# Decode attention with a gated MLP on one core: the rest of w2 loaded last, its products summed with wo's, and other sizes for the last value parts

## The chip, the cores and the metric

One Trainium2 chip, of which the kernel uses one core. The metric is the device time of one execution in microseconds, the median of several runs; lower is better.

## The reference

One token x (512 numbers) goes through two branches, and a gate mixes them. All tensors are bf16.

```python
g = sigmoid((x * gate_w).sum(-1))
q = (x @ wq).reshape(32 heads, 128)
scores = einsum("hd,hkd->hk", q, k_cache) * 128 ** -0.5     # 32 heads x 4096 positions
o = einsum("hk,hkd->hd", softmax(scores), v_cache)
a = o.reshape(4096) @ wo                                    # 4096 x 512
h = relu(x @ w1 + b1) ** 2                                  # 512 x 1376
b = h @ w2 + b2                                             # 1376 x 512
out = g * a + (1 - g) * b
```

The key and value caches are 32 x 4096 x 128 each, 67 MB together. wq and wo have 4 MB each, w1 and w2 1.4 MB each.

## The kernel before

There is no scheduler: each engine's program is written out by hand, and semaphores order the engines.

**Tiles.** Four heads make one tile of 4 MB (128 partitions x 128 blocks of 128 numbers), so there are NT = 8 key tiles and 8 value tiles. All of them, and the MLP's weights ("m"), pass through a ring of five slots in SBUF, `ring`, in the order of `LOADS`: k0, k1, k2, v0, k3, v1, and so on to k7, v5, v6, m, v7. SyncE (SP) issues these loads in that order (L319 to L338); before each it waits until the tile that had the slot is used up. The last three value tiles are loaded in parts with a semaphore each; `PARTS` holds where they are cut. For the last one these are blocks 0, 40, 76, 108, 128: parts of 40, 36, 32 and 20 blocks. One block is 128 x 128 numbers of bf16, 32 KB. Behind the last value part SP issues the last four heads' rows of wo in two pieces, three heads and one head (L340), and at the very end the store of the result.

**Scores and probabilities.** VectorE (DVE) computes 20 of each 32 blocks' scores with a fused multiply and sum (L716). TensorE (PE) transposes the other blocks (L509) and multiplies them with q (L524), with ScalarE (ACT) copying between. The maximum over a head goes over PE and DVE, ACT takes the exponentials (L434) and their sums.

**Values.** `pv(u)` multiplies blocks of a value tile with the probabilities (L555) and sums them in PSUM. `norm` (L746) divides by the sum of probabilities and multiplies by the gate g; the result is `onorm`.

**The end of the program on PE.** After the value products of tile 6:

- `turn_a`, `spread_a`, `out_a`: the first 28 heads are turned over and multiplied with 22 of the 32 parts of their rows of wo (L585, 88 products into `acc`, which is pQ[:, 256:260]).
- `mlp_h`: first MLP layer. The 1376 hidden units are 10 columns of 128 and a rest of FR = 96; per column four products (L600) into `H`.
- `den` (L564), then `mlp_out`: second MLP layer, 44 products (L612) into a PSUM region of its own, `MO`. The last four use `w2b`, the 96 rows of the rest of w2. `mlp_out` waits for both loads of w2 (`s_w[1]`, `s_w[2]`) and for `hs`.
- `pv` of the last value tile, in four steps that are its four parts. Between the first and the second, `add_v` (L591) adds the sum of the other ten parts of wo, which DVE computes itself (L777, L781).
- `out_b`: the last four heads times their rows of wo (L621, 12 and 4 products into `acc`); then the transpose of the final result.

On DVE, `mlp_bias` and `mlp` add b1, square the positive part and multiply by 1 - g (`omg`, one number per partition) to give `hs` (L756, L761, L765). Behind the sums for wo come the reciprocal, the sum of `MO` and the bias (L817), `norm` of the last group, the sum with `acc` (L821) and a copy (L823).

**At the start** SP and GpSimd may go on with wo's loads once q is computed and the bias b1 has been turned into columns (`started`); b1 goes over PE (L468) and two DVE copies into `b1c` (L700, L701).

Of the kernel before, what the change touches and what calls it, by code (L numbers as in the profile page):

```python
# [5 lines left out]
def bass_gated_mix__gqa_block_cached__dense_activation_squared_relu__decode_kernel(  # L6
# [15 lines left out]
    fp32 = mybir.dt.float32  # L22
    bf16 = mybir.dt.bfloat16
    ALU = mybir.AluOpType
# [5 lines left out]
    DM = 512  # L30
    F = 1376
    FG = 10
    FR = F - FG * 128
    SCALE = float(D) ** -0.5


# [2 lines left out]
    NT = NH // R  # L39
    B = 4096 // P  # L40
# [16 lines left out]
    PV[NU - 2] = [NU - 3 * U, NU - 3 * U + 1]  # L57
    PV[NU] = list(range(NU - 3 * U + 2, NU - U))

    PARTS = {NT - 3: [0, 64, B], NT - 2: [0, 32, 64, 96, B], NT - 1: [0, 40, 76, 108, B]}  # L60

    GR = [(0, 8), (8, 16), (16, 24), (24, 28), (28, 32)]
    NG = len(GR)
# [7 lines left out]
    NA = 28  # L71
    NZ = NH - NA
    TS = [0, 3, NZ]
# [59 lines left out]
    with ctx:  # L133
        def sb(name, shape, dt):
            return ctx.enter_context(nc.sbuf_tensor(name, shape, dt))
# [4 lines left out]
        def sem(name):  # L140
            return ctx.enter_context(nc.semaphore(name))
# [3 lines left out]
        def held(kind, j=0):  # L145
            return ring[:, AT[kind, j] % SLOTS, :]
# [4 lines left out]
        W2, W3 = 4 * F, 4 * F + FG * DM  # L151
        w1_sb = held("m")[:, 0:W2].rearrange("p (t n) -> p t n", t=4)
        w2a = held("m")[:, W2:W3].rearrange("p (g n) -> p g n", g=FG)
        w2b = held("m")[0:FR, W3:W3 + DM]
        W4 = W3 + DM
        W5 = W4 + NZ * DM
        wob_sb = held("m")[:, W4:W5].rearrange("p (h n) -> p h n", h=NZ)
# [4 lines left out]
        start = ring[:, SLOTS - 1, :]  # L162
# [6 lines left out]
        xrow, grow, b1r, b2r = early(1, DM), early(1, DM), early(1, F), early(4, 128)  # L169
# [5 lines left out]
        xcol = sb("xcol", [128, 4], bf16)  # L175
        xcolf = sb("xcolf", [128, 4], fp32)
        b1c = sb("b1c", [128, FG + 1], fp32)
# [17 lines left out]
        onorm = sb("onorm", [128, NH], bf16)  # L195
# [4 lines left out]
        omg = sb("omg", [128, 1], fp32)  # L200
        hr = sb("hr", [128, FG + 1], fp32)
        hp = sb("hp", [128, FG + 1], fp32)
        hs = sb("hs", [128, FG + 1], bf16)
        b2g = sb("b2g", [128, 4], fp32)
        fin = sb("fin", [128, 4], bf16)

# [4 lines left out]
        pX = pb("pX", [128, 512], fp32)  # L211
# [9 lines left out]
        B2 = KP[2][:, 0:4]  # L221
        QR = [pQ, pX]
        H = pX[:, 256:256 + FG + 1]
        MO = pX[:, 288:292]
        B1 = pM[:, 288:288 + FG + 1]
        acc = pQ[:, 256:260]

# [50 lines left out]
        s_rd = sem("s_rd")  # L278
        s_on = sem("s_on")
        s_h = sem("s_h")  # L280
        s_mo = sem("s_mo")
        s_fb = sem("s_fb")
        s_vs = sem("s_vs")
        s_hv = sem("s_hv")
        s_hs = sem("s_hs")
# [25 lines left out]
        def started(eng):  # L311
            eng.wait_ge(s_qps, NT)
            eng.wait_ge(s_g, 4)
            eng.wait_ge(s_b1c, 2)


        @block.sync
        def _(eng):
            for n, (kind, j) in enumerate(LOADS):  # L319
                free(eng, n)  # L320
                if n == SLOTS - 1:
                    started(eng)
                    for p, st, k, q in STRIPS[len(RUNS):]:
                        a, b = W[p:p + st * (k - 1) + 1:st, :], woa_v[q:q + k, :]
                        if k == 1:
                            a, b = [v.rearrange("p (a n) -> p a n", a=2) for v in (a, b)]
                        eng.dma_start(a, b).then_inc(s_wr, 16)
                if kind == "v" and j in PARTS:
                    for w in range(len(PARTS[j]) - 1):
                        part = slice(PARTS[j][w] * 128, PARTS[j][w + 1] * 128)  # L330
                        eng.dma_start(held("v", j)[:, part], v_v[j][:, part]).then_inc(s_vl[j, w], 16)  # L331
                elif kind in "kv":
                    eng.dma_start(held(kind, j), (k_v if kind == "k" else v_v)[j])\
                       .then_inc(s_l[n % SLOTS], 16)
                elif kind == "m":
                    eng.dma_start(held("m")[:, 0:W2], w1_v).then_inc(s_w[0], 16)
                    eng.dma_start(held("m")[:, W2:W3], w2_v).then_inc(s_w[1], 16)  # L337
                    eng.dma_start(w2b, B_w2[FG * 128:F, :]).then_inc(s_w[2], 16)  # L338
            for c in range(len(TS) - 1):
                eng.dma_start(wob_sb[:, TS[c]:TS[c + 1], :], wob_v[:, TS[c]:TS[c + 1], :])\  # L340
                   .then_inc(s_wo[c], 16)
            eng.wait_ge(s_f4, 1)
            eng.dma_start(out[0, 0, :].rearrange("(j p) -> j p", p=128), fin4).then_inc(s_out, 16)

# [109 lines left out]
        def _(eng):  # L454
# [9 lines left out]
            eng.wait_ge(s_b, 32)  # L464
            eng.transpose(B2, b2r, ident[0:4, 0:4]).then_inc(s_b2, 1)
            for n in range(FG + 1):
                M = 128 if n < FG else FR
                mm = eng.matmul(B1[0:M, n:n + 1], b1r[:, n:FG * 128:FG] if n < FG else b1r[:, FG * 128:F],  # L468
                                ident[0:1, 0:1], start=True, stop=True)
            mm.then_inc(s_b1, 1)  # L470
            eng.wait_ge(s_wq, 16)
# [1 line left out]
            eng.wait_ge(s_ez, 1)  # L473


            read = [(s_b1c, 2)]

            def pm(sem, count):
                for w in read:
# [114 lines left out]
            def mlp_h():  # L594
                eng.wait_ge(s_w[0], 16)
                for n in range(FG + 1):
                    M = 128 if n < FG else FR
                    for t in range(4):
                        lhs = w1_sb[:, t, n:FG * 128:FG] if n < FG else w1_sb[:, t, FG * 128:F]
                        mm = eng.matmul(H[0:M, n:n + 1], lhs, xcol[:, t:t + 1],  # L600
                                        start=(t == 0), stop=(t == 3))
                mm.then_inc(s_h, 1)

            def mlp_out():
                eng.wait_ge(s_w[1], 16)
                eng.wait_ge(s_w[2], 16)
                eng.wait_ge(s_hs, 1)
                for n in range(FG + 1):
                    M = 128 if n < FG else FR
                    w = w2a[:, n, :] if n < FG else w2b  # L610
                    for j in range(4):
                        mm = eng.matmul(MO[:, j:j + 1], w[:, j * 128:(j + 1) * 128], hs[0:M, n:n + 1],  # L612
                                        start=(n == 0 and j == 0), stop=(n == FG and j == 3),
                                        skip_group_check=True)
                mm.then_inc(s_mo, 1)

            def out_b(c):
                eng.wait_ge(s_wo[c], 16)
                for h in range(TS[c], TS[c + 1]):
                    for j in range(4):  # L620
                        mm = eng.matmul(acc[:, j:j + 1], wob_sb[:, h, j * 128:(j + 1) * 128],  # L621
                                        onorm[:, NA + h:NA + h + 1], start=False, stop=(h == NZ - 1),
                                        skip_group_check=True)
                if c == len(TS) - 2:
                    mm.then_inc(s_acc, 1)

            for c in range(EARLY):
                q_rows(c)
# [33 lines left out]
            max_cols(NT - 1)  # L662
            mlp_h()
            den(NG - 1)
            mlp_out()
            for u in range((NT - 1) * U, NU):
                if u == NU - 3:
                    add_v()
# [1 line left out]
            eng.wait_ge(s_on, NG)  # L670
            for c in range(len(TS) - 1):
                out_b(c)
            eng.wait_ge(s_fin, 1)
            eng.transpose(KP[2][0:4, 0:128], fin[:, :], ident[:, :]).then_inc(s_fT, 1)

# [1 line left out]
        @block.vector  # L677
        def _(eng):
            eng.memset(zeros, 0.0).then_inc(s_dz, 1)
            eng.memset(b1c[:, :], 0.0).then_inc(s_dz, 1)  # L680
            eng.wait_ge(s_dz, 2)
            eng.wait_ge(s_x, 32)
            eng.tensor_tensor_reduce(grow, xrow, grow, 1.0, 0.0, ALU.mult,
                                     ALU.add, zp[:, :]).then_inc(s_zp, 1)
# [12 lines left out]
            eng.tensor_scalar(b2g[:, :], B2, omg[:, 0:1], None, ALU.mult).then_inc(s_g, 1)  # L697

            eng.wait_ge(s_b1, 1)
            eng.tensor_copy(b1c[:, 0:FG], B1[:, 0:FG]).then_inc(s_b1c, 1)  # L700
            eng.tensor_copy(b1c[0:FR, FG:FG + 1], B1[0:FR, FG:FG + 1]).then_inc(s_b1c, 1)  # L701

            def qcol_copy(c):
                eng.wait_ge(s_q, c + 1)
# [46 lines left out]

            def mlp_bias():
                eng.wait_ge(s_h, 1)
                eng.wait_ge(s_b1c, 2)
                for p, n in cells:
                    eng.tensor_tensor(hr[p, n], H[p, n], b1c[p, n], ALU.add).then_inc(s_hv, 1)  # L756

            def mlp():
                eng.wait_ge(s_hv, 1)
                for p, n in cells:  # L760
                    eng.scalar_tensor_tensor(out=hp[p, n], in0=hr[p, n], scalar=0.0, in1=hr[p, n],  # L761
                                             op0=ALU.max, op1=ALU.mult).then_inc(s_hv, 1)
                eng.wait_ge(s_hv, 2)
                for p, n in cells:
                    eng.tensor_scalar(hs[p, n], hp[p, n], omg[p, 0:1], None, ALU.mult).then_inc(s_hs, 1)  # L765

            def rows_v():
                eng.wait_ge(s_ac, 3)
# [43 lines left out]
            gmax(NT - 1)  # L812
            rows_v()
            recip(NG - 1)
            eng.wait_ge(s_mo, 1)
            eng.wait_ge(s_g, 4)
            eng.tensor_tensor(b2g[:, :], MO, b2g[:, :], ALU.add).then_inc(s_fb, 1)  # L817
            norm(NG - 1)
            eng.wait_ge(s_acc, 1)
            eng.wait_ge(s_fb, 1)  # L820
            eng.tensor_tensor(fin[:, :], acc[:, 0:4], b2g[:, :], ALU.add).then_inc(s_fin, 1)  # L821
            eng.wait_ge(s_fT, 1)
            eng.tensor_copy(fin4, KP[2][0:4, 0:128]).then_inc(s_f4, 1)  # L823
# [31 lines left out]
```

## Time and profile before

| What | Value |
|---|---|
| Median of 3 runs | 193.54 us (193.41 to 193.6) |
| The profiled execution | 193.49 us |
| Its span, first to last instruction | 192.1 us |
| Mean granted TensorE clock | 0.595 |
| Busy: PE, DVE, ACT, POOL | 109.9, 158.8, 82.7, 22.9 us |
| Moved by DMA | 78.71 MB, mean 410 GB/s |

All times below are microseconds from the start of the span. A profile line such as "L555 PE MATMUL pO<-E,ring 128*128 128x4 bf16 x20" names the source line, the engine, what is written and read, the shape, and how many such instructions are merged in the row; PEld is TensorE's weight load, SPq and DVEq the sequencers of their engines. In brackets stands how long the engine had been idle before, and what ended that. "us to landing" of a DMA runs from its issue to the last of its semaphore's increments.

### The profile page before, as it was taken

The page shows a single profiled execution, that of the slowest core. Times are in us where ns is not written, and L with a number is a line of the kernel's source. Part 1 is how long each engine was busy: PE and PEld are TensorE (multiplying, and loading weights), DVE is VectorE, ACT ScalarE, POOL GpSimd, SP SyncE. Part 2 cuts the span into 40 slices and gives each one's busy share as a digit, 9 for nine tenths or more (in the row PEclk, how much of TensorE's full clock was granted, in tenths as well). Part 3 has the DMA queues.
Part 4 walks back from the last instruction along what each step waited for, and adds up shares of the span by engine and source line. Part 5 has one row for each costly group of instructions (what it writes and reads, how often), then busy time and mean ns, then how long its engine had stood idle before and what let it go on. Part 6 is the DMA issues. An engine that isn't in the chain of part 4 may idle for free.

```text
span 192.1 us, 6035 instructions
## 1 busy us (share of the span) xinstructions
PE 109.9 (57%) x2056; PEld 97.1 (51%) x2058; DVE 158.8 (83%) x1387; ACT 82.7 (43%) x204; POOL 22.9 (12%) x56
## 2 busy tenths in 40 slices
PE   0139665544614653397469255935876488449884
PEld 0123344434513542297459145924876378448873
DVE  0310299999999999999999998998999799998721
ACT  2104776743833663078339232933744383001300
POOL 7760000995000000000000000000000000000000
PEclk9999999555555555555555555555855555555555
DMA  6999999999999999999999999999999999999991
GB/s 225 431 437 437 437 438 426 432 438 432 423 428 416 423 432 413 447 404 433 416 432 416 440 428 437 425 421 437 420 421 416 406 426 411 422 418 382 407 386 68
DMA packets 5456, 78.71 MB, mean 410 GB/s; under 512 B 1285, under 2 KB 1895, under 8 KB 2024
## 3 DMA queue, kind: packets, MB, share of 16 engines
q1 hardware_dynamic: 4452, 75.37, 92.9%
q0 software_dynamic: 960, 2.95, 3.8%
q8 instruction: 16, 0.26, 0.6%
q14 instruction: 14, 0.11, 0.1%
q10 hardware_dynamic: 14, 0.01, 0.0%
HBM read 78.32 MB, written 0.00 MB: 408 GB/s over the span
## 4 chain that ended last, share of the span: by engine, by line
DVE 48%; DMA 41%; SPq 6%; PE 3%; issue 1%; DVEq 0%
DVE ring L716 45%; DMA ring<-in_A_k_cache_dram 26%; DMA ring<-in_A_v_cache_dram 15%; SPq L331 5%; DVE S L716 2%; PE pO L555 1%; PE KP L509 1%; DVE gm L730 1%; DVE gx L733 0%; PE pQ L621 0%; PE pM L564 0%; PE pM L536 0%; SPq L337 0%; SPq L338 0%; SPq L294 0%
## 5 line engine op out<-in xcount | busy, mean ns | idle before, releaser
L716 DVE CUSTOM_DVE_ANT_0 ring<-ring,qb 128x128 bf16<-128x128 bf16 x656 | 140.6, 283 | 2.4 <-DMA ring<-in_A_k_cache_dram 2.4
L415 ACT ACTIVATE kT<-KP 128x768 bf16<-128x768 bf16 (+1 forms) x64 | 46.4, 783 | 48.7 <-PE KP L509 48.4
L509 PE MATMUL KP<-ident,ring 128*128 128x128 bf16 x368 | 43.0, 300 | 21.8 <-DMA ring<-in_A_k_cache_dram 18.6
L716 DVE DVE_READ_ACCUMULATOR2_ANT S<- 128x1 f32 x656 | 51.8, 79 | 0.1
L509 PEld LDWEIGHTS KP<-ident,ring 128*128 128x128 bf16 x368 | 35.6, 139 | 23.9 <-DMA ring<-in_A_k_cache_dram 19.0
L555 PE MATMUL pO<-E,ring 128*128 128x4 bf16 x640 | 19.8, 166 | 2.8 <-DMA ring<-in_A_v_cache_dram 2.2
L555 PEld LDWEIGHTS pO<-E,ring 128*128 128x128 bf16 x640 | 18.9, 105 | 3.4 <-DMA ring<-in_A_v_cache_dram 2.4
L434 ACT ACTIVATE E<-S,nM 32x128 bf16<-32x128 f32 x32 | 18.5, 579 | 0.9
L555 PE MATMUL pX<-E,ring 128*128 128x4 bf16 x384 | 11.9, 166 | 4.7 <-DMA ring<-in_A_v_cache_dram 4.7
L555 PEld LDWEIGHTS pX<-E,ring 128*128 128x128 bf16 x384 | 11.3, 103 | 5.2 <-DMA ring<-in_A_v_cache_dram 5.1
L426 ACT ACTIVATE nM<-pM 128x1 f32<-128x1 f32 x8 | 1.4, 170 | 23.0 <-PE pM L536 23.0
L531 PE MATMUL pM<-identf,mp 128*1 128x128 f32 x8 | 3.1, 384 | 13.9 <-DVE mp L723 13.9
L536 PE MATMUL pM<-onesf,gx 1*128 1x1 f32 x16 | 4.5, 345 | 9.1 <-DVE gx L733 9.1
L536 PEld LDWEIGHTS pM<-onesf,gx 1*128 1x128 f32 x16 | 3.8, 291 | 9.8 <-DVE gx L733 9.7
L524 PE MATMUL pQ<-qcol,kT 128*128 128x4 bf16 x176 | 7.8, 170 | 1.0 <-ACT kT L415 0.9
L531 PEld LDWEIGHTS pM<-identf,mp 128*1 128x1 f32 x8 | 0.7, 91 | 15.2 <-DVE mp L723 15.0
L524 PEld LDWEIGHTS pQ<-qcol,kT 128*128 128x128 bf16 x176 | 7.6, 111 | 1.3 <-ACT kT L415 1.3
L434 ACT ACTIVATION_READ_ACCUMULATOR E<-S,nM 32x1 f32 x32 | 8.1, 253 | 0.0
L386 POOL MEMSET tick<- 1x1 f32 x1 | 0.1, 90 | 66.9 <-DMA W<-in_A_wo_dram 66.9
L378 POOL DMA_DIRECT2D W<-in_A_wo_dram x14 | 8.0, 574 | 0.0
L524 PE MATMUL pS<-qcol,kT 128*128 128x4 bf16 x192 | 7.8, 168 | 0.0
L363 POOL TENSOR_SCALAR_AFFINE_SELECT selA<-selA 28x36 bf16<-28x36 bf16 (+6 forms) x22 | 7.4, 335 | 3.2 <-POOL selA L358 0.2
(83 smaller groups left out, 97.6 us busy)
## 6 DMA issues: line engine op xcount, KB each, us to landing
ring<-in_A_k_cache_dram SPq DMA_DIRECT2D x8, 4096.0 KB, 30.1
ring<-in_A_v_cache_dram SPq DMA_DIRECT2D x5, 4096.0 KB, 29.2
ring<-in_A_v_cache_dram SPq DMA_DIRECT2D x5, 1024.0 KB, 28.8
W<-in_A_wq_dram SPq DMA_DIRECT2D x1, 4096.0 KB, 12.6
ring<-in_A_v_cache_dram SPq DMA_DIRECT2D x2, 2048.0 KB, 27.5
W<-in_A_wo_dram POOLq DMA_DIRECT2D x2, 768.0 KB, 18.2
ring<-in_B_w_dram SPq DMA_DIRECT2D x1, 1376.0 KB, 25.0
ring<-in_B_w_dram SPq DMA_DIRECT2D x1, 1280.0 KB, 28.2
```

What stands on the lines that cost most here:

```text
L331: eng.dma_start(held("v", j)[:, part], v_v[j][:, part]).then_inc(s_vl[j, w], 16)
L363: eng.affine_select(out=part, in_=part, compare_op=ALU.not_equal, fill=1.0, base=-st * q, pattern=[[st, 4], [-1, st * (k - 1) + 1]], chann ...
L378: eng.dma_start(W[p:p + st * (k - 1) + 1:st, :], woa_v[q:q + k, :], max_dma_last_dim=16384).then_inc(s_wp[n], 16)
L415: eng.activation(kT[:, n % NC, 0:HB[u // U] * 128], KP[n % 3][:, 0:HB[u // U] * 128], ACT.Copy).then_inc(s_ev, 1)
L434: eng.activation(E[rows, j % NE, :, r], S[rows, j % NS, :], ACT.Exp, bias=nM[rows, j:j + 1], scale=SCALE, accum_out=RS[rows, R * j + r:R * ...
L509: mm = eng.transpose(KP[n % 3][:, y * 128:(y + 1) * 128], held("k", j)[:, b * 128:(b + 1) * 128], ident[:, :])
L524: mm = eng.matmul(S2[j % 2][:, c:c + R], kT[:, n % NC, y * 128:(y + 1) * 128], qcol[:, R * j:R * j + R], start=True, stop=True)
L531: eng.transpose(MT[0:1, :], mp[:, j:j + 1], identf[:, :]).then_inc(s_mt, 1)
L536: eng.matmul(MB[:, j:j + 1], gx[0:1, j % 2, :], onesf[0:1, 0:1], start=True, stop=True).then_inc(s_mb, 1)
L555: mm = eng.matmul(O(R * j, R * j + R), held("v", j)[:, b * 128:(b + 1) * 128], E[:, j % NE, b, :], start=(b == 0), stop=(b == B - 1), skip ...
L716: ins = eng.tensor_tensor_reduce(kb, kb, qb[:, j, :], 1.0, 0.0, ALU.mult, ALU.add, S[:, j % NS, b:b + 1])
L730: eng.tensor_reduce(g, MT[0:1, :].rearrange("a (r p) -> a r p", r=R), AX.X, ALU.max)\
```

## The change

Three things are edited together.

1. The rest of w2. `w2b` takes all 128 partitions: it now holds the last 128 rows of w2 (rows 1248 to 1375). The first 32 of these are also in the ten full columns, so they must count with weight zero here. For that, w1's last column and b1's are widened in the same way to the last 128 hidden units, and a new tile `omw` holds 1 - g for every cell but the first FO = 32 partitions of the last column, where it is 0. `hs` is the product with `omw`. The load moves from behind the main part of w2 to behind the two pieces of wo: it is the last load that SP issues.
2. The second MLP layer has no PSUM region of its own any more. Its products go into `acc`. The 40 of the full columns stand where all 44 stood; the four of the rest stand behind `out_b`, ahead of the final transpose, and wait for the moved load. The sum of `MO` and the bias on DVE is gone.
3. The last value tile is cut at 0, 40, 80, 116, 128: parts of 40, 40, 36 and 12 blocks.

```diff
+    FO = 128 - FR
...
-    PARTS = {NT - 3: [0, 64, B], NT - 2: [0, 32, 64, 96, B], NT - 1: [0, 40, 76, 108, B]}
+    PARTS = {NT - 3: [0, 64, B], NT - 2: [0, 32, 64, 96, B], NT - 1: [0, 40, 80, 116, B]}
...
-        w2b = held("m")[0:FR, W3:W3 + DM]
+        w2b = held("m")[:, W3:W3 + DM]
...
+        omw = sb("omw", [128, FG + 1], fp32)
...
-        MO = pX[:, 288:292]
...
         def started(eng):
...
-            eng.wait_ge(s_b1c, 2)
+            eng.wait_ge(s_b1c, 1)
...
                     eng.dma_start(held("m")[:, W2:W3], w2_v).then_inc(s_w[1], 16)
-                    eng.dma_start(w2b, B_w2[FG * 128:F, :]).then_inc(s_w[2], 16)
             for c in range(len(TS) - 1):
                 eng.dma_start(wob_sb[:, TS[c]:TS[c + 1], :], wob_v[:, TS[c]:TS[c + 1], :])\
                    .then_inc(s_wo[c], 16)
+            eng.dma_start(w2b, B_w2[F - 128:F, :]).then_inc(s_w[2], 16)
...
             for n in range(FG + 1):
-                M = 128 if n < FG else FR
-                mm = eng.matmul(B1[0:M, n:n + 1], b1r[:, n:FG * 128:FG] if n < FG else b1r[:, FG * 128:F],
+                mm = eng.matmul(B1[:, n:n + 1], b1r[:, n:FG * 128:FG] if n < FG else b1r[:, F - 128:F],
                                 ident[0:1, 0:1], start=True, stop=True)
...
                     for t in range(4):
-                        lhs = w1_sb[:, t, n:FG * 128:FG] if n < FG else w1_sb[:, t, FG * 128:F]
-                        mm = eng.matmul(H[0:M, n:n + 1], lhs, xcol[:, t:t + 1],
+                        lhs = w1_sb[:, t, n:FG * 128:FG] if n < FG else w1_sb[:, t, F - 128:F]
+                        mm = eng.matmul(H[:, n:n + 1], lhs, xcol[:, t:t + 1],
...
-            def mlp_out():
-                eng.wait_ge(s_w[1], 16)
-                eng.wait_ge(s_w[2], 16)
-                eng.wait_ge(s_hs, 1)
-                for n in range(FG + 1):
...
+            def mlp_out(n):
+                if n in (0, FG):
+                    eng.wait_ge(s_w[1 if n < FG else 2], 16)
+                if n == 0:
+                    eng.wait_ge(s_hs, 1)
+                w = w2a[:, n, :] if n < FG else w2b
+                for j in range(4):
+                    mm = eng.matmul(acc[:, j:j + 1], w[:, j * 128:(j + 1) * 128], hs[:, n:n + 1],
+                                    start=False, stop=(n == FG), skip_group_check=True)
+                if n == FG:
+                    mm.then_inc(s_acc, 1)
...
             den(NG - 1)
-            mlp_out()
+            for n in range(FG):
+                mlp_out(n)
             for u in range((NT - 1) * U, NU):
                 if u == NU - 3:
                     add_v()
...
             for c in range(len(TS) - 1):
                 out_b(c)
+            mlp_out(FG)
             eng.wait_ge(s_fin, 1)
...
         @block.vector
         def _(eng):
             eng.memset(zeros, 0.0).then_inc(s_dz, 1)
-            eng.memset(b1c[:, :], 0.0).then_inc(s_dz, 1)
+            eng.memset(omw[:, :], 1.0).then_inc(s_dz, 1)
             eng.wait_ge(s_dz, 2)
+            eng.memset(omw[0:FO, FG:FG + 1], 0.0).then_inc(s_dz, 1)
...
             eng.wait_ge(s_b1, 1)
-            eng.tensor_copy(b1c[:, 0:FG], B1[:, 0:FG]).then_inc(s_b1c, 1)
-            eng.tensor_copy(b1c[0:FR, FG:FG + 1], B1[0:FR, FG:FG + 1]).then_inc(s_b1c, 1)
+            eng.tensor_copy(b1c[:, :], B1).then_inc(s_b1c, 1)
+            eng.wait_ge(s_dz, 3)
+            eng.tensor_scalar(omw[:, :], omw[:, :], omg[:, 0:1], None, ALU.mult).then_inc(s_g, 1)
...
                 eng.wait_ge(s_hv, 2)
+                eng.wait_ge(s_g, 5)
                 for p, n in cells:
-                    eng.tensor_scalar(hs[p, n], hp[p, n], omg[p, 0:1], None, ALU.mult).then_inc(s_hs, 1)
+                    eng.tensor_tensor(hs[p, n], hp[p, n], omw[p, n], ALU.mult).then_inc(s_hs, 1)
...
-            eng.wait_ge(s_mo, 1)
-            eng.wait_ge(s_g, 4)
-            eng.tensor_tensor(b2g[:, :], MO, b2g[:, :], ALU.add).then_inc(s_fb, 1)
             norm(NG - 1)
             eng.wait_ge(s_acc, 1)
-            eng.wait_ge(s_fb, 1)
+            eng.wait_ge(s_g, 4)
             eng.tensor_tensor(fin[:, :], acc[:, 0:4], b2g[:, :], ALU.add).then_inc(s_fin, 1)
```

More of the change, by code (lines that the diff above doesn't have):

```diff
@@ L280, in bass_gated_mix__gqa_block_cached__dense_activation_squared_relu__decode_kernel @@
         s_h = sem("s_h")
-        s_mo = sem("s_mo")
-        s_fb = sem("s_fb")
         s_vs = sem("s_vs")
@@ L473, in _ @@
             eng.wait_ge(s_ez, 1)
-            read = [(s_b1c, 2)]
+            read = [(s_b1c, 1)]
             def pm(sem, count):
@@ L596, in mlp_h @@
                 for n in range(FG + 1):
-                    M = 128 if n < FG else FR
                     for t in range(4):
-                        lhs = w1_sb[:, t, n:FG * 128:FG] if n < FG else w1_sb[:, t, FG * 128:F]
-                        mm = eng.matmul(H[0:M, n:n + 1], lhs, xcol[:, t:t + 1],
+                        lhs = w1_sb[:, t, n:FG * 128:FG] if n < FG else w1_sb[:, t, F - 128:F]
+                        mm = eng.matmul(H[:, n:n + 1], lhs, xcol[:, t:t + 1],
                                         start=(t == 0), stop=(t == 3))
                 mm.then_inc(s_h, 1)
-            def mlp_out():
-                eng.wait_ge(s_w[1], 16)
-                eng.wait_ge(s_w[2], 16)
-                eng.wait_ge(s_hs, 1)
-                for n in range(FG + 1):
[L609 to L615, printed above, removed]
+            def mlp_out(n):
[9 more added lines that the diff above has]
+                    mm.then_inc(s_acc, 1)
             def out_b(c):
@@ L620, in out_b @@
                     for j in range(4):
[L621 to L625, printed above, removed]
+                        eng.matmul(acc[:, j:j + 1], wob_sb[:, h, j * 128:(j + 1) * 128],
+                                   onorm[:, NA + h:NA + h + 1], start=False, stop=False,
+                                   skip_group_check=True)
             for c in range(EARLY):
@@ L753, in mlp_bias @@
                 eng.wait_ge(s_h, 1)
-                eng.wait_ge(s_b1c, 2)
+                eng.wait_ge(s_b1c, 1)
                 for p, n in cells:
```

## Prediction

> **What bounds the kernel now.** I read the page's header, its slices and queues first, then the chain that ended last, then the DMA issues of the last 42 us, then the timelines of SP, PE and DVE there. The page says that the 16 DMA engines are full from the second slice to the last but one:
>
> ```profile
> span 192.1 us, 6035 instructions
> ...
> DMA  6999999999999999999999999999999999999991
> ...
> q8 instruction: 16, 0.26, 0.6%
> ```
>
> So the bytes set when the last value tile has landed, and the end follows from there. The tail of the chain in order of time (start, length, what) shows that path:
>
> ```profile
> 150.45 0.43 SPq L338
> 150.93 2.44 SPq L331
> 153.41 4.63 SPq L331
> 158.08 2.10 SPq L331
> 160.22 28.18 DMA ring<-in_A_v_cache_dram
> 188.40 0.05 issue
> 188.45 0.71 PE pO L555 x20
> ...
> 189.25 0.23 DVE onorm L746
> ...
> 189.54 0.58 PE pQ L621 x16
> ...
> 190.15 0.17 DVE fin L821
> ...
> 190.37 0.28 PE KP L674
> ...
> 190.67 0.21 DVE ring L823
> ```
>
> The fourth part of the last value tile lands at 188.40. After it stand 20 blocks on PE, the normalisation, wo's 16 products (over at 189.54 + 0.58 = 190.12), the bias, a transpose, a copy and the store. What does not stand in the chain is how near the other transfers are. The DMA issues from 150 us on give size and time from issue to landing, and SP's timeline the issue of the two wo pieces (162.00, and 167.03 for the second, whose issue lasts 7.62 us to 174.65):
>
> ```profile
> ring<-in_A_v_cache_dram SPq DMA_DIRECT2D x1, 1280.0 KB, 30.6
> ring<-in_A_v_cache_dram SPq DMA_DIRECT2D x1, 1152.0 KB, 30.9
> ring<-in_A_v_cache_dram SPq DMA_DIRECT2D x1, 1024.0 KB, 28.8
> ring<-in_A_v_cache_dram SPq DMA_DIRECT2D x1, 640.0 KB, 28.2
> ring<-in_A_wo_dram SPq DMA_DIRECT2D x1, 384.0 KB, 27.4
> ring<-in_A_wo_dram SPq DMA_DIRECT2D x1, 128.0 KB, 22.7
> ring<-in_B_w_dram SPq DMA_DIRECT2D x1, 96.0 KB, 28.1
> ```
>
> ```profile
> 162.00 12.64 SPq L340 DMA_DIRECT2D ring<-in_A_wo_dram  x2
> ```
>
> ```profile
> 167.03 7.62 SPq L340 DMA_DIRECT2D ring<-in_A_wo_dram  x1
> ```
>
> PE's rows from 180 us give the pace of its products: seven more cost 1.21 - 1.02 = 0.19 us, so one starts 0.027 us behind another, and the last takes about 0.17 us by itself:
>
> ```profile
> 180.67 1.31 PE L612 MATMUL pX<-hs,ring 128*128 128x1 bf16 x44
> 181.84 1.21 PE L555 MATMUL pO<-E,ring 128*128 128x4 bf16 x40
> 183.43 1.87 PE L591 MATMUL pQ<-onesf,ring 128*128 128x1 f32 x8 [0.38 <-DVE ring L781]
> 185.16 1.02 PE L555 MATMUL pO<-E,ring 128*128 128x4 bf16 x33
> 186.66 1.25 PE L555 MATMUL pO<-E,ring 128*128 128x4 bf16 x35 [0.48 <-issue]
> ```
>
> Issue plus flight gives the landings. Value parts: 150.93 + 30.6 = 181.5, 153.41 + 30.9 = 184.3, 158.08 + 28.8 = 186.9, and 188.4. wo: 162.00 + 27.4 = 189.40 and 167.03 + 22.7 = 189.73. The rest of w2: 150.45 + 28.1 = 178.55. So the DMA stream itself ends at 189.73, only 0.39 us before wo's products end. They start at 189.54, when the first wo piece has been there for 0.14 us; the thirteenth, the first that needs the second piece, comes about 12 x 0.027 us later, at 189.86, 0.13 us after that piece. Two limits, the value chain and the end of the stream, lie almost on top of each other. That is the whole case.
>
> **Part 1: the rest of w2, 96 rows early to 128 rows last.** The price of bytes at this place: from 188.40 to 189.73 the stream moved 512 KB of wo in rows of 1 KB, 1.33 us, or 0.33 us for 128 KB and 0.25 us for 96 KB. From the first value part to the fourth (181.5 to 188.4) 2816 KB took 6.9 us, which gives 0.31 and 0.24. I take the wo row, since it has the same row length. So everything behind the old place lands 0.25 us earlier: value part four at 188.15, wo at 189.15 and 189.48. The new load then ends the stream at 189.48 + 0.33 = 189.81, 0.08 us (32 KB) later than the stream ends now. A bound from the other side is the old load itself. With
>
> ```profile
> 149.96 0.45 SPq L337
> ```
>
> ```profile
> ring<-in_B_w_dram SPq DMA_DIRECT2D x1, 1280.0 KB, 28.2
> ```
>
> the main part of w2 landed at 178.16 and the rest at 178.55, 0.39 us for 96 KB, which would make 0.52 us of 128 KB. Combining either end for what is taken out (0.24 to 0.39) with either for what is put in (0.31 to 0.52), the stream ends between 189.65 and 190.01.
>
> On SP's queue, 0.43 us of issue goes from ahead of the value parts. This gains nothing: each part is in flight for 28 us and more, so an earlier issue only stands longer in line. The new issue is behind wo's, at 174.65. If it lasts as long as the longest of these rows, 7.62 us, it is done at 182.3, seven us before its turn.
>
> **Part 2: parts of 40, 40, 36 and 12 blocks.** The bytes are the same. Twelve blocks are 384 KB; the present 20 blocks took 188.4 - 186.9 = 1.5 us, so part three now lands 0.9 us before part four, at 187.24. From 187.24 + 0.05 the 36 + 12 blocks run in one piece: 47 x 0.027 + 0.17 = 1.44 us, to 188.73. They no longer wait for part four at 188.15. The value chain thus ends 0.43 us earlier than the 188.45 + 0.71 = 189.16 of now, and from there to wo's first product it is 189.54 - 189.16 = 0.38 us as before: ready at 189.11. But wo's first piece lands at 189.15, so the products start at 189.20.
>
> The 0.48 us of "issue" before 186.66 is PE waiting for nothing that the profile shows, three blocks short of the end of part two. With four products moved behind, about the same place of the program (72 products from its end) is three blocks short of the end of the new part two, whose third part lands at 187.24: 0.5 us of cover behind 186.75, when those three blocks are done. The Trainium skill ("Runtime: NRT & Kernel Launch", "Instruction fetch mechanics") says that instructions come in blocks of 16 KiB, 256 of them, and that crossing into the next is mostly hidden. Here the page's queue of instructions moved 16 packets in 0.26 MB, which agrees in size; the idle 0.48 us, if it is that crossing, was not hidden from PE.
>
> **Part 3: the second layer summed with wo's products.** 40 of 44 products stay where they are; four (0.11 us) go behind wo's. The value tile's first part starts 0.11 us earlier, and the wait for DVE's sum at 183.43 takes that back. What counts is the new last wait: the four products need the load of part 1. 189.81 + 0.05 + 3 x 0.027 + 0.17 = 190.11. Behind the waiting PE only the final transpose is queued. Against 190.12 before: zero. The sixteen wo products, started at 189.20, are issued by 189.64 and hide under that wait.
>
> **Part 4: VectorE and the start.**
>
> ```profile
> 180.12 0.23 DVE L765 TENSOR_SCALAR hs<-hp,omg 128x11 bf16<-128x11 f32 x1
> 183.38 0.13 DVE L817 TENSOR_TENSOR b2g<-pX,b2g 128x4 f32<-128x4 f32 x1
> 189.25 0.22 DVE L746 SCALAR_TENSOR_TENSOR onorm<-pO,gcol,rden 128x4 bf16<-128x4 f32 x1 [5.73 <-PE pO L555]
> ```
>
> ```profile
> 0.90 0.07 DVE L680 MEMSET b1c<- 128x11 f32 x1
> 13.90 0.14 DVE L701 COPY b1c<-pM 96x1 f32<-96x1 f32 x1
> 17.38 0.16 DVE L705 CAST qcol<-pM 128x4 bf16<-128x4 f32 x1 [3.33 <-PE pM L494]
> ```
>
> The add at L817 goes, in front of 5.73 us of waiting: nothing. Its cover gone, it would be worth 0.13 us. The product for hs becomes one of two tensors, between the 0.13 us of L817's form and the 0.23 of now, beside the same wait. At the start a copy (0.14) goes, and a small fill (0.07) and a product on 128x11 (at most the 0.23 of L765) come: +0.16 us in front of 3.33 us of waiting for PE. The new wait for that product is met 160 us before it is asked. The bias and first layer over 128 rows instead of 96 keep their instruction count. All this is zero.
>
> **Sum.** End of the products 190.11 for 190.12; all behind it is as it was. The profiled run took 193.49 us around a span of 192.1, 0.05 under the median of the runs, 193.54. With the bounds of part 1 the products end between 189.95 and 190.31, so -0.2 to +0.2 us. I say 193.55.
>
> **Rivals.** *The stream's end does not bind (faster).* If the last load lands by 189.5, the value chain alone decides: 20 products from 189.11, 19 x 0.027 + 0.17, end 189.79, or -0.33 us: 193.2. With the larger price of the removed load (0.39) everything is 0.14 earlier still, -0.47: 193.1. For it speaks that the old load cost more than its bytes; against it, that all bytes are still there and 32 KB more, with engines that show no empty slice. Chance 0.18, two thirds of it beyond 0.2%.
>
> *A refill of instructions on the DMA engine that finishes last (slower).* 16 KB on one engine, at the 8 KB per engine in 0.33 us of the wo row, delay it by 0.66 us; the queue's 0.6% share over 16 packets makes 1.15 us of each. In the new order PE has no slack behind the end of the stream, so such a packet would show in full: 194.2 to 194.7. It decides once it holds the last load beyond 190.2. Against it: PE runs the same number of instructions, so refills should fall at the same places. Chance 0.14.
>
> *The last load comes too late into the line (slower).* Its issue begins at 174.65. If it were held past 189.3, the queue would run dry and the load would pay its whole flight: the store at the end, issued at
>
> ```profile
> 190.91 0.29 SPq L343 DMA_DIRECT2D out_dram<-ring  x1
> ```
>
> and the last thing in the span of 192.1, shows 1.2 us for 1 KB. That gives about +1.2 us: 194.7. For it, issues grow (2.44 and 4.63 us for value parts, 5.0 and 7.62 for wo); against, it would have to last 14.6 us. Chance 0.08. The Trainium skill ("DMA: Bandwidth & Descriptors", "Anatomy of one DMA — SWDGE (gpsimd) path") fits a DMA issued by GpSimd as 2.0 us plus its bytes at 436 GB/s, and so speaks against a small load at the end: 2.3 us by an estimate from it, against the 0.33 us of the equal wo piece. The rows show that nearly all the fixed part hides in a full line, so the rule bites only in this rival.
>
> **Chances.** The forecast has 0.60, with a range of its own of 193.35 to 193.75, the -0.2 to +0.2 us of the sum. 0.2% is 0.39 us, about what a measurement of this kernel can tell from no change. Faster: 0.12. Same: 0.60 + 0.06 = 0.66. Slower: 0.14 + 0.08 = 0.22. The range runs from the fast rival's end, 193.1, to the near price of the refill, 194.2, and leaves out the dear half of the slow rivals.
>
> **What would show it.** Right: the fourth value part lands about 188.15 and PE goes from part three into it without a gap; wo's products start near 189.2; then PE idles some 0.2 us with the load of w2 as releaser, and its last four products end near 190.1. Wrong: no idle time there (the fast rival), or a last landing after 190.2. The sum of part 1 is wrong if the last load lands more than 0.5 us after wo's second piece.

## The result, and the profile after

The changed kernel takes 192.95 us (median of 7 runs, 192.78 to 193.18) where the kernel before takes 193.54 (7 runs): the ratio is 0.9974, with a 95% interval of 0.9963 to 0.9985. It is faster by 0.26%, or about 0.5 us. The forecast was no change, 193.55, with a low end of 193.1. The gain was not forecast, and the time lies below the range.

In the profiled execution the span went from 192.1 to 191.6 us. The chain that ended last, from 184 us on (start, length, what):

```profile
162.66 25.98 DMA ring<-in_A_wo_dram
188.64 0.14 issue
188.78 0.56 PE pQ L618 x16
189.34 0.28 PE pQ L609 x4
189.62 0.02 issue
189.65 0.17 DVE fin L818
```

The products end at 189.62 instead of 190.12. The first sixteen now wait for wo's first piece (188.64), not for the value chain, and the last four, as shown further below, for the last load. SP's issues and the flights of the DMAs that stand behind this (each flight is added to its issue):

```profile
149.86 0.33 SPq L336
150.23 0.43 SPq L337
...
153.65 3.94 SPq L331
157.63 4.99 SPq L331
```

```profile
172.33 2.64 SPq L341 DMA_DIRECT2D ring<-in_B_w_dram  x1
```

```profile
ring<-in_B_w_dram SPq DMA_DIRECT2D x1, 1376.0 KB, 24.8
ring<-in_B_w_dram SPq DMA_DIRECT2D x1, 1280.0 KB, 27.6
ring<-in_A_v_cache_dram SPq DMA_DIRECT2D x1, 1152.0 KB, 33.1
ring<-in_A_v_cache_dram SPq DMA_DIRECT2D x1, 384.0 KB, 30.1
...
ring<-in_B_w_dram SPq DMA_DIRECT2D x1, 128.0 KB, 17.0
```

The fourth value part lands at 157.63 + 30.1 = 187.7 and the last load at 172.33 + 17.0 = 189.3. Before, the corresponding landings were 188.40 and, for the last piece of wo, 189.73. The stream carries 32 KB more and ends 0.4 us earlier. Where that time was lost before shows in three stretches of both kernels. The columns are the stretch and its length, busy time of PE, PEld, DVE, ACT and POOL (with the number of instructions), the granted clock, the mean busy share of the DMA engines and GB/s. First the kernel before, then the changed one:

```profile
168.00:174.00 6.00, 2.99 (x73) 2.31 (x74) 5.23 (x46) 0.00 (x0) 0.00 (x0) 0.50 1.01 418
174.00:180.00 6.00, 5.68 (x134) 5.56 (x134) 4.79 (x10) 2.54 (x9) 0.00 (x0) 0.50 1.02 381
180.00:184.00 4.00, 3.40 (x89) 3.31 (x89) 3.37 (x8) 0.00 (x0) 0.00 (x0) 0.50 1.00 418
```

```profile
168.00:174.00 6.00, 2.90 (x70) 2.22 (x70) 5.40 (x50) 0.00 (x0) 0.00 (x0) 0.50 1.01 420
174.00:180.00 6.00, 5.77 (x135) 5.66 (x136) 4.98 (x11) 2.54 (x9) 0.00 (x0) 0.50 1.01 421
180.00:184.00 4.00, 3.35 (x86) 3.24 (x86) 3.18 (x6) 0.00 (x0) 0.00 (x0) 0.50 1.00 418
```

Before, the 96 packets of 1 KB of the load to 96 partitions run from 174.3 to 178.0 us. From 174 to 180 us the DMA engines were as busy as ever (1.02) and moved 381 GB/s instead of 421. That is (421 - 381) x 6 = 240 KB less, or 0.57 us of the stream. The page of the kernel before has the same dip in its row of rates, in the 37th slice (172.9 to 177.7 us):

```profile
GB/s 225 431 437 437 437 438 426 432 438 432 423 428 416 423 432 413 447 404 433 416 432 416 440 428 437 425 421 437 420 421 416 406 426 411 422 418 382 407 386 68
```

The packet records of the traces say which packets were slow: not the small ones (0.048 to 0.052 us each in the mean) but the 10 KB packets of the transfers around them. Such a packet took 0.389 us in the mean from 173 to 174 us and 0.486 us from 175 to 176; in the changed kernel it is 0.387 to 0.389 in each microsecond from 172 to 178.

### The profile page after: what moved, and what is told of

Read it like the earlier page. It is cut to its first block, busy times and chain, and to the rows that moved or that the text cites. A ratio compares the mean times of both kernels' runs of the same rounds, so it can differ in the third digit from the quotient of the medians.

```text
span 191.6 us, 6036 instructions
## 1 busy us (share of the span) xinstructions
PE 110.1 (57%) x2058; PEld 97.4 (51%) x2058; DVE 158.9 (83%) x1387; ACT 82.7 (43%) x204; POOL 22.8 (12%) x56
## 4 chain that ended last, share of the span: by engine, by line
DVE 48%; DMA 40%; SPq 7%; PE 3%; issue 1%; DVEq 0%
DVE ring L715 45%; DMA ring<-in_A_k_cache_dram 26%; DMA ring<-in_A_wo_dram 14%; SPq L331 6%; DVE S L715 2%; PE pO L554 1%; PE KP L508 1%; DVE gm L729 1%; DVE gx L732 0%; PE pM L535 0%; PE pM L563 0%; PE pQ L618 0%; SPq L337 0%; SPq L294 0%; SPq L336 0%
## 5 line engine op out<-in xcount | busy, mean ns | idle before, releaser
L715 DVE DVE_READ_ACCUMULATOR2_ANT S<- 128x1 f32 x656 | 50.7, 77 | 0.1
L406 ACT ACTIVATE qb<-pQ 32x128 bf16<-32x128 f32 x16 | 4.3, 268 | 8.1 <-PE pQ L486 7.8
## 6 DMA issues: line engine op xcount, KB each, us to landing
ring<-in_A_v_cache_dram SPq DMA_DIRECT2D x4, 1024.0 KB, 27.6
ring<-in_B_w_dram SPq DMA_DIRECT2D x1, 1376.0 KB, 24.8
```

The lines of the kernel that those rows point to most:

```text
L406: eng.activation(qb[rows, c, :], QR[c % 2][rows, r * 128:r * 128 + 128], ACT.Copy)\
L715: ins = eng.tensor_tensor_reduce(kb, kb, qb[:, j, :], 1.0, 0.0, ALU.mult, ALU.add, S[:, j % NS, b:b + 1])
```

## The experiments

Theories after the result: **shape** (a load to 96 partitions slows the transfers around it), **place** (short rows amid long ones are dear), **parts** (the shorter last value part brings the gain). All ratios are to the kernel before on the same chip, where its median was 193.33 to 193.54. The last column is the time from the landing of w1 to that of value part four in the profiled execution: in all runs the main part of w2 and the last value tile land in it, and besides only what is loaded of the rest of w2 ahead of that part.

| Run | Median, us | Ratio (95% interval) | GB/s, 174 to 180 us | w1 to value part four, us |
|---|---|---|---|---|
| kernel before | 193.33 to 193.54 | 1 | 381 | 13.79 |
| changed kernel | 192.95 | 0.9974 (0.9963 to 0.9985) | 421 | 13.01 |
| early128 | 193.23 | 0.9985 (0.9976 to 0.9994) | 417 | 13.34 |
| rows128_same_bytes | 193.06 | 0.9975 (0.9966 to 0.9984) | 416 | 13.28 |
| parts_only | 193.45 | 0.9991 (0.9982 to 1.0) | 383 | 13.66 |
| last96 | 192.93 | 0.9969 (0.9956 to 0.9981) | 424 | 13.01 |
| rows64_same_bytes | 193.58 | 1.0006 (0.9997 to 1.0015) | 372 | 13.93 |
| twice96 | 194.05 | 1.0038 (1.0025 to 1.0051) | 341 | 14.56 |
| plus128 | 193.67 | 1.0011 (1.0002 to 1.002) | 382 | 14.08 |
| old_parts | 192.95 | 0.9972 (0.9961 to 0.9983) | 420 | 13.01 |
| amid96 | 193.4 | 1.0001 (0.9992 to 1.0009) | 404 | 13.70 |
| rows32_same_bytes | 193.6 | 1.0009 (1.0 to 1.0018) | 362 | 14.05 |
| rows16 | 193.92 | 1.0026 (1.0017 to 1.0035) | 362 | 14.20 |
| rows64_step2 | 192.86 | 0.9972 (0.9962 to 0.9983) | 418 | 13.29 |

The last column gives the price of the load itself. The three kernels that have it behind value part four take 13.01 us. The 96 rows of the kernel before add 0.78 us (0.65 in parts_only, which has the same load); the same 96 KB over 128 partitions add 0.27, and 128 KB over 128 partitions add 0.33.

### Shape against place

**early128**, the changed kernel with

```diff
+                    eng.dma_start(w2b, B_w2[F - 128:F, :]).then_inc(s_w[2], 16)   # behind the main part of w2
-            eng.dma_start(w2b, B_w2[F - 128:F, :]).then_inc(s_w[2], 16)           # behind wo
```

> The changed kernel with one thing undone: the rest of w2, still 128 rows to 128 partitions, is loaded at its old place behind the main part of w2. Shape theory (a load to 96 partitions slows the transfers around it; one to 128 costs only its bytes, 0.33 us): the four value parts land 0.33 us later than in the changed kernel, the end of the stream stays, the last products end about 0.1 us later: 193.0 to 193.1. Place theory (rows of 1 KB amid rows of 10 KB are dear, at the end they are not): the gain is lost, 193.5.

About half the gain stays, 0.15%, and the rate hardly dips (417). So place alone does not explain the loss; but the gain is less than the shape theory gave. Its price of the load was right (0.33 us in the last column); its end of the products was not. wo's first piece stands behind the load here, and its landing ends the wait at 189.25; 20 products follow it without a gap, where the kernel before had 16:

```profile
189.25 0.56 PE L618 MATMUL pQ<-onorm,ring 128*128 128x1 bf16 x16 [0.56 <-DMA ring<-in_A_wo_dram]
189.68 0.24 PE L609 MATMUL pQ<-hs,ring 128*128 128x1 bf16 x4
```

**rows128_same_bytes**, the kernel before with

```diff
-                    eng.dma_start(w2b, B_w2[FG * 128:F, :]).then_inc(s_w[2], 16)
+                    eng.dma_start(held("m")[:, W3:W3 + 384], <the same 96 x 512 numbers as 128 x 384>).then_inc(s_w[2], 16)
```

> The kernel before with one thing changed: the 96 KB of the rest of w2 are loaded at the old place as 128 partitions x 768 B instead of 96 x 1024 B. The numbers so lie wrong for the second layer's last four products; all instructions stay. Shape theory: the load costs 0.25 us instead of about 0.8, so 193.0. Place theory: rows are even shorter, no gain: 193.5 or a little more. In the shape theory the main part of w2 also lands some 0.3 us earlier than in the kernel before, 3.1 us behind w1 instead of 3.4 (mean over the DMA engines).

One line of the kernel before, the same bytes at the same place, and the whole gain is there: 0.9975. The products of value part four then start at 188.03 and not at 188.45:

```profile
162.63 25.35 DMA ring<-in_A_v_cache_dram
187.98 0.05 issue
188.03 0.70 PE pO L556 x20
```

This is the run that settles shape against place for the old place.

**last96**, the changed kernel with the rest of w2 as 96 rows again:

```diff
-        w2b = held("m")[:, W3:W3 + DM]
+        w2b = held("m")[0:FR, W3:W3 + DM]
...
-            eng.dma_start(w2b, B_w2[F - 128:F, :]).then_inc(s_w[2], 16)
+            eng.dma_start(w2b, B_w2[FG * 128:F, :]).then_inc(s_w[2], 16)
```

> The changed kernel with 96 rows to 96 partitions instead of 128, loaded last all the same; products and their place as in the changed kernel. Place theory: 32 KB less at the end, 192.9. Shape theory: the load now slows wo's pieces and itself, so that the gain is in part lost, 193.1 to 193.5, with the last landing 0.5 us or more behind wo's second piece instead of 0.32.

A miss for the shape theory: at the end of the stream 96 rows cost nothing, 0.9969, and they land 0.18 us behind wo's second piece, not the 0.5 us or more that this theory gave. So either edit is enough, the shape or the place.

**amid96**, last96 with the load moved up between two value parts:

```diff
                         eng.dma_start(held("v", j)[:, part], v_v[j][:, part]).then_inc(s_vl[j, w], 16)
+                        if j == NT - 1 and w == 0:
+                            eng.dma_start(w2b, B_w2[FG * 128:F, :]).then_inc(s_w[2], 16)
```

> The changed kernel with 96 rows to 96 partitions, and that load moved from the end of the stream to between the first and the second part of the last value tile. If such a load is dear wherever the other engines move long rows to all partitions: the 0.5 us over its bytes come back, 193.35 to 193.5, with a dip of the rate around its landing. If only the old place (behind w1 and the main part of w2) was dear: 192.95, as with the same load at the end.

The gain is gone, 1.0001; the load adds 0.69 us to the 13.01 of last96, and the dip moves with it: 404 from 174 to 180 us and now also 399 from 180 to 184 us, where last96 has 417:

```profile
180.00:184.00 4.00, 3.17 (x85) 3.02 (x85) 3.18 (x6) 0.00 (x0) 0.00 (x0) 0.50 0.99 399
```

So it is not the neighbourhood of w1 and w2. At both places tried where the stream runs full with long rows, this load is dear.

### The dose

**twice96** and **plus128**, the kernel before with one more load behind the first, into a spare part of the tile:

```diff
+                    eng.dma_start(spare[0:FR, :], B_w2[FG * 128:F, :]).then_inc(s_w[2], 16)      # twice96
+                    eng.dma_start(spare[:, :], B_w2[F - 128:F, :]).then_inc(s_w[2], 16)          # plus128
```

> The kernel before with the load of 96 rows issued a second time, into a spare part of the tile; the second layer waits for both. Shape theory: as much again as the 0.7 to 0.8 us that the first one takes from the stream, 194.2 to 194.3. By bytes: 0.25 us, 193.75.

> The kernel before with a load of 128 rows x 1024 B added behind the one of 96 rows, into a spare part of the tile; the second layer waits for both. Shape theory: its bytes alone, 0.33 us: 193.85. Theory that any rows of 1 KB amid long ones are dear: 1 us, 194.5.

A second load of 96 KB to 96 partitions costs 0.38%, 0.73 us; one of 128 KB to 128 partitions costs 0.11%, 0.2 us. By the medians alone it is 0.62 and 0.24 us, by the last column 0.77 and 0.29. Per byte the first is thus three to five times as dear. Rows of 1 KB are not what is dear.

### Which partitions

**rows64_same_bytes**, **rows32_same_bytes**, **rows16** and **rows64_step2**, the kernel before with the load reshaped, into a spare part of the tile:

```diff
-                    eng.dma_start(w2b, B_w2[FG * 128:F, :]).then_inc(s_w[2], 16)
+                    eng.dma_start(spare[0:64, :],    <96 KB as 64 x 768>).then_inc(s_w[2], 16)     # rows64_same_bytes
+                    eng.dma_start(spare[0:32, :],    <96 KB as 32 x 1536>).then_inc(s_w[2], 16)    # rows32_same_bytes
+                    eng.dma_start(spare[0:16, :],    <90 KB as 16 x 2880>).then_inc(s_w[2], 16)    # rows16
+                    eng.dma_start(spare[0:127:2, :], <96 KB as 64 x 768>).then_inc(s_w[2], 16)     # rows64_step2
```

> The kernel before with one thing changed: the 96 KB of the rest of w2 are loaded at the old place as 64 partitions x 1536 B, into a spare part of the tile. The second layer's last four products read what is left there from before; all instructions stay. Port theory (a load that does not cover all 128 partitions makes DMA engines write through the ports of others, which are busy): as dear as with 96 rows or more, 193.5 to 193.9, and the main part of w2 lands 3.4 us behind w1 or more. If something of the number 96 alone were dear: 193.05, as with 128 partitions.

> The kernel before with the 96 KB of the rest of w2 loaded at the old place as 32 partitions x 3072 B into a spare part of the tile; the second layer's last four products read what is left in their place. If the ports decide, and 32 partitions lie on the same eight ports as 64: as with 64 rows, 193.45 to 193.75. If the number of partitions decides: dearer than 64 rows by as much as these were over 128, 194.0.

> The kernel before with 90 KB of the rest of w2 loaded at the old place as 16 partitions x 5760 B into a spare part of the tile; the second layer's last four products read what is left in their place. If the ports decide: 16 partitions lie on four of them, the load is dearer than with 32 or 64, 193.7 to 194.2, and the packets around it last longer at the peak. If only the rows below 128 matter: 193.5.

> The kernel before with the 96 KB of the rest of w2 loaded at the old place as 64 rows x 1536 B, as in the run with 64 partitions, but to every second partition (0, 2, ... 126) of a spare part of the tile, so that all sixteen ports get four rows each; the second layer's last four products read what is left in their place. If the load of the ports decides: nearly as cheap as 128 rows, 193.05 to 193.25, and the rate from 174 to 180 us stays above 405 GB/s. If the number of rows decides, or that an engine writes to a port that another one is writing to: as dear as 64 partitions in one piece, 193.5 to 193.7.

64 partitions in one piece are at least as dear as 96 (1.0006), 32 not measurably more than 64 in time (1.0009), 16 more (1.0026, with 6% fewer bytes). In the last column these loads add 0.92, 1.04 and 1.19 us. The decisive pair is 64 partitions against 64: the same rows of the same length, but on every second partition, give 0.9972 and add 0.28 us, as much as 128 partitions do. The rates from 174 to 180 us, first in one piece, then with a step of two:

```profile
174.00:180.00 6.00, 5.53 (x132) 5.42 (x128) 4.80 (x10) 2.54 (x9) 0.00 (x0) 0.50 1.02 372
```

```profile
174.00:180.00 6.00, 5.84 (x135) 5.72 (x134) 4.79 (x10) 2.54 (x9) 0.00 (x0) 0.50 1.01 418
```

The 10 KB packets that start from 174 to 178 us take 0.468 us in the mean in the first and 0.390 in the second. So neither the number of rows nor their length decides, but how evenly a load lies over the partitions. The Trainium skill ("SBUF — State Buffer", "Door 1: The DMA port swizzle (why `[64,N]` ≈ `[32,N]`)") gives a mechanism: sixteen DMA ports with eight partitions each; partitions 0 to 63 lie on eight of them, 0 to 31 on the same eight, 0 to 15 on four, and by its table every second partition reaches all sixteen evenly, while 0 to 95 put twice as many rows on each of eight ports as on each of the others. The order of these runs agrees with that. That section of the Trainium skill speaks of the bandwidth of such a load itself; that the packets of the loads around it slow down is what the packet times above show. The ports themselves are in no trace here.

### The parts

**parts_only** is the kernel before with the new cut, **old_parts** the changed kernel with the old one:

```diff
-    PARTS = {..., NT - 1: [0, 40, 76, 108, B]}
+    PARTS = {..., NT - 1: [0, 40, 80, 116, B]}     # parts_only; old_parts is the reverse, in the changed kernel
```

> The kernel before with only the last value tile cut into 40, 40, 36 and 12 blocks. Parts theory (the gain comes from the shorter last part): 193.0. Shape theory: wo's landings stay where they are (189.40, 189.73) and its products can start only 0.1 us earlier: 193.4 to 193.55.

> The changed kernel with the last value tile cut as before, into 40, 36, 32 and 20 blocks. Twenty blocks from the landing at 187.7 end at 188.45 instead of 188.28, so wo's products start 0.1 to 0.2 us later: 193.05 to 193.15. If the parts had brought the gain: 193.5.

The cut alone brings 0.09%, with an interval that reaches from 0.18% to nothing, and taken out of the changed kernel it costs nothing (0.9972 against 0.9974). The forecast of 0.1 to 0.2 us for old_parts was a miss. Its PE rows show why:

```profile
187.82 0.70 PE L554 MATMUL pO<-E,ring 128*128 128x4 bf16 x20 [0.31 <-DMA ring<-in_A_v_cache_dram]
188.91 0.59 PE L618 MATMUL pQ<-onorm,ring 128*128 128x1 bf16 x16 [0.39 <-DVE onorm L745]
189.39 0.27 PE L609 MATMUL pQ<-hs,ring 128*128 128x1 bf16 x4
```

The products start 0.13 us later than in the changed kernel (188.91 against 188.78), but the last four start at 189.39 against 189.34, since in the changed kernel they waited 0.13 us for the last load in any case (see part 3 below).

## Why the prediction was wrong

**Where it failed: part 1, the price of what is taken out.** I took 0.25 us, with 0.39 as the upper end, and the load really took 0.78 us from the stream in these traces: value part four lands 13.79 us behind w1 before and 13.01 in the changed kernel. The bytes were priced at the end of the stream, from wo's rows, which go to all partitions. For a load to 128 partitions that price was right (0.27 us in rows128_same_bytes); what it missed is what the shape does to the transfers around the load. The upper end was the distance between two landings, the main part of w2 and its rest. That distance is not the price, since the load had already slowed the transfer ahead of it: the main part of w2 landed 178.16 - (149.59 + 25.0) = 3.6 us behind w1 before, and (150.23 + 27.6) - (149.86 + 24.8) = 3.2 us behind it in the changed kernel. These 0.4 us and the load's own 0.39 make 0.8 (0.50 and 0.31 from the unrounded landings). The price of what is put in was right: the last load of the changed kernel landed 0.32 us behind wo's second piece in the trace, against 0.33. So the stream's end moved by -0.43 us instead of +0.08.

The rows that gave w1's landing before:

```profile
149.59 0.33 SPq L336
```

```profile
ring<-in_B_w_dram SPq DMA_DIRECT2D x1, 1376.0 KB, 25.0
```

I took it that engines without an empty slice move data at the full rate. The row of rates under the busy shares said 382 where its neighbours said 418 and 407.

**Part 2** was right in its form. Parts three and four run as one piece, and the values are done 0.57 us behind the fourth part's landing, where old_parts needs 0.75; but other waits hide this, and the time does not change with it. The piece shows in the rows below: the first has the three blocks left of part two and the 36 + 12 behind them.

```profile
186.76 1.52 PE L554 MATMUL pO<-E,ring 128*128 128x4 bf16 x51 [0.65 <-issue]
188.78 0.56 PE L618 MATMUL pQ<-onorm,ring 128*128 128x1 bf16 x16 [0.50 <-DMA ring<-in_A_wo_dram]
189.34 0.27 PE L609 MATMUL pQ<-hs,ring 128*128 128x1 bf16 x4
```

The idle time marked "issue" lies three blocks short of the end of part two, as worked out, but 0.65 us long, and its cover is gone: part three has landed at 153.65 + 33.1 = 186.75 when it ends at 186.76. From there PE, not the landing of values, sets when the normalisation comes.

**Part 3** was right about the last wait: the four products wait for the last load. The rows hide it, since the profile models the ends of products. The sixteen start 0.027 us apart from 188.78 on, so the four could follow at 189.21, 0.43 us behind the first, as they do in early128 (189.25 and 189.68). They start at 189.34, 0.04 us behind the load's landing. That is 0.13 us of waiting where I took 0.2. wo's products start 0.14 us behind their landing where I took 0.05. The end of the stream still sets the end of the program, 0.43 us earlier than before. **Part 4** shows in none of the rows that wait.

**The rivals.** The fast rival had the right side and the right reason in its favour ("the old load cost more than its bytes"). Its largest number, -0.47, lies near the 0.50 us by which the products of the two profiled executions differ, but that is in part luck: it priced the load at 0.39 and let the value chain alone decide, and here PE waited for wo and for the last load. Neither slow rival came: the last load's issue ended at 172.33 + 2.64 = 174.97, and among the packets ahead of the last landing there is no refill of instructions, though one ran beside them from 187.86 us on.

**What stays open:** why 96 rows cost nothing at the end of the stream (last96). Fewer DMA engines are at work there: in the changed kernel their busy share is 0.89 from 184 to 188 us, and the sixteen increments of the last load's semaphore come from 186.47 to 189.30. That this, or the short rows there, is the reason is argued, not shown.

## What to carry to other kernels

In a kernel bound by its DMA stream, look at the rate beside the busy share, and look for loads that do not lie evenly on all 128 partitions wherever the rate dips. Spread such a load over all partitions (128 KB over 128 partitions took 0.33 us, 96 KB over 96 took 0.78), or try it at the very end of the stream; here one reshaped load was worth as much as the whole change. And price a transfer by what the stream does with and without it, not by the distance between its landing and the one ahead.

## What the runs showed of the hardware

A load of 96 KB to 64 or 96 neighbouring partitions lowered the rate of the whole stream from about 420 to 372 and 381 GB/s over 6 us, with the DMA engines' busy share at 1.02. With 96 partitions the 10 KB packets of the loads around it went from 0.389 to 0.486 us, and the load took 0.78 us from the stream, against 0.27 for the same bytes over 128 partitions. The same 64 rows on every second partition left 418 GB/s.
